# A third PSUM tile for the first MLP layer, a new order of fills, and earlier loads in a fused attention and MLP kernel

## The chip, the cores and the metric

One core of a Trainium2 chip. The metric is the device time of one execution in microseconds (us), the median of several. Executions fall into states: most agree closely, and some are several us longer; comparisons between kernels use the fast ones.

## The reference

Attention with a hash mask, then an MLP on its output, in float32:

```python
# q, k, v: (4 batches, 8 heads, 768, 64); proj: (64, 6)
q_bits = (q @ proj > 0); k_bits = (k @ proj > 0)     # 6 bits a token
mask   = bucket(q_bits)[:, None] == bucket(k_bits)[None, :]
attn   = softmax(where(mask, q @ k.T / 8, -1e9))
x      = (attn @ v) as (3072 tokens, 512)
h      = x @ w_in                                    # (3072, 2048): first layer
out    = (h * cos(h)) @ w_out                        # (3072, 512):  second layer
```

## The kernel before

The work runs in 192 units of attention, 48 a batch: TensorE (PE) makes scores in one of two tiles `s_ps` of PSUM (where its results land), ScalarE (ACT) takes the exp, PE multiplies by the values into `av_ps`. Two heads share one load ("pair"); pair n is loaded, cast, transposed and hashed some units before it is needed. Seven units into batch b, the *first layer* of batch b-1 runs: 16 rounds, one for each `ff`, of eight matmuls, cos on ACT, and the product h·cos on VectorE (DVE). The *second layer* of that batch, 96 matmuls of 512 columns in 6 row tiles of 16, is spread as "fills" over the following units and over the next first layer. The first layers of batches 1 and 2 are called the middle ones below: they have fills, that of batch 0 has none, that of batch 3 stands alone at the end.

```python
    s_ps = [psp.tile([P, 2, 512], FP32, ...) for i in range(2)]   # scores and first layer
    av_ps = [psp.tile([P, 512], FP32, ...) for i in range(2)]     # values, by head parity
    m_ps = [psp.tile([P, 512], FP32, ...) for i in range(2)]      # second layer, in turn
    ...
    def l1_ff(b, ff, hp):
        halves = hp if isinstance(hp, list) else [hp[:, c, :] for c in range(2)]
        for ft in range(NFT):
            for c in range(2):
                nc.tensor.matmul(out=halves[c][:, 0:C2], lhsT=win_t[ft][:, ff * P:(ff + 1) * P],
                    rhs=xT[(b, ft)][:, 3 * c:3 * c + 3, :], start=(ft == 0), stop=(ft == NFT - 1))
        ...                                    # ACT: cos; DVE: g = h * cos
    def l2_mm():
        b, qt, ff = l2q.pop(0)
        if ff == 0:
            state["m"] = 1 - state["m"]        # each row tile takes the other bank
        o_ps = m_ps[state["m"]]
        ...
        nc.tensor.matmul(out=o_ps, lhsT=g[:, qt * P:(qt + 1) * P], rhs=wout_t[ff],
            start=(ff == 0), stop=(ff == NFF - 1))
        if ff == NFF - 1:
            ...
            nc.vector.tensor_copy(out=ob, in_=o_ps)     # then the row tile goes out
            nc.sync.dma_start(out=dst, in_=ob)
    ...
            if n < NEARLY:                     # NEARLY = 5, UB = 48
                at(s0 + 2, lambda n=n: load(n + 2, nc.sync if n + 2 < NEARLY else nc.gpsimd))
            elif NEARLY < n < NP - 1:
                at(max(s0 - 1, UB + 8), lambda n=n: load(n + 1, nc.gpsimd))
    ...
    L1_AT = {UB * b + 7: b - 1 for b in range(1, B)}
    for u in range(U):
        score(h, jt); ...                      # exp, values, and what is due at this unit
        if b > 0:
            fill(2 if (u % 3 == 0) else 1)
        if u in L1_AT:
            bb = L1_AT[u]
            for ff in range(NFF):
                if bb == 0 and ff % 3 == 2:
                    hp = m_ps
                else:
                    hp = s_ps[state["rot"] % 2]
                    state["rot"] += 1
                l1_ff(bb, ff, hp)
                if bb == 0:
                    nc.gpsimd.tensor_copy(out=mark, in_=g_tiles[(0, ff)][:, 0, 0:1])
                    weights_out(ff)            # one of 16 w_out pieces
                if ff in (0, 1) and len(pend) > 0:
                    av_step()
                if bb > 0:
                    fill(2)
            l2_add(bb)
            fill(5)
```

Pairs from 5 on are transposed by DMA on the SyncE queue, while the loads come from GpSimd (POOL). DVE must copy the transposed keys (`kx<-qx`) before it makes the blocks of the next pair (`blkq`, `blkk`: its queries and keys, rearranged for the hash), and PE runs that hash between two units.

The softmax here doesn't subtract the row's maximum and nothing guards it: scores larger than these inputs give would overflow.

## Time and profile before

| | before |
|---|---|
| median, first three runs | 320.37 us (326.35, 320.37, 319.7) |
| profiled execution | 325.93 us, span 324.2 us, slow |
| PE busy in the profile | 309.6 us, 96% |
| middle first layers | 16 rounds of 1.73 us |
| longest wait of PE | 4.59 us, at 105 us |

The page of the profile: busy time of each engine, then the busy tenths and the granted clock of PE in 40 slices of the span.

```profile
span 324.2 us, 7617 instructions
...
PE 309.6 (96%) x3074; PEld 183.7 (57%) x3074; DVE 179.2 (55%) x376; ACT 231.1 (71%) x278; POOL 107.2 (33%) x180
...
PE   8899999999999499999999999999999999999995
...
PEclk9999999999999689999999999999999999999999
```

PE is full nearly everywhere. The exception is the 14th slice (from 105.4 us), where it is busy for less than half of the time; there and in the next its clock is below full. The same stretch in the chain of work that ended last, in order of time (start, duration, what):

```profile
95.37 12.17 DMA qx<-n16x
...
107.57 0.04 DVE kx L235
...
107.84 0.68 DVE ob L336
...
108.55 0.99 DVE blkq L143
...
109.59 0.85 PE m_ps L156 x2
```

Read downward, this is one wait: a DMA transpose lands at 107.5 us, only then can DVE copy the keys, empty an output bank and make the blocks of the next pair, and only then PE begins the hash. The timeline shows the parts on POOL (the natq load of pairs 7, 8, 9 and 10), SyncE (the transposes), DVE (the first key copy), PE and ACT; the columns are start, duration, engine, line, operation, tiles, count, and in brackets the idle time before and what ended it:

```profile
83.75 0.72 POOL L100 DMA_DIRECT2D natq<-in_q_dram  x1
...
85.87 0.74 POOL L100 DMA_DIRECT2D natq<-in_q_dram  x1
...
93.17 0.73 POOL L100 DMA_DIRECT2D natq<-in_q_dram  x1
...
101.22 0.72 POOL L100 DMA_DIRECT2D natq<-in_q_dram  x1
...
93.88 3.95 SPq L230 DMA_TRANSPOSE qx<-n16x  x2
...
105.53 0.35 DVE L235 COPY kx<-qx 64x768 f16<-64x768 f16 x1 [6.35 <-DMA qx<-n16x]
...
109.59 0.85 PE L156 MATMUL m_ps<-blkq,projblk 128*32 128x192 f32 x2 [4.59 <-DVE blkq L143]
...
95.81 10.00 ACT L250 ACTIVATE pt<-s_ps,exp_bias 128x768 f16<-128x768 f32 x12 [0.93 <-PE s_ps L244]
113.65 0.90 ACT L250 ACTIVATE pt<-s_ps,exp_bias 128x768 f16<-128x768 f32 x1 [7.84 <-PE s_ps L244]
```

An undisturbed hash costs ACT a pause of 0.93 us (the line at 95.81); this one costs 7.84. The second cause beside the wait is the clock, here a stretch of two us from the view of stretches (the columns are the stretch, its length, busy time of PE, PEld, DVE, ACT and POOL, then the granted clock, 0.50, and the DMA share and rate):

```profile
112.00:114.00 2.00, 2.00 (x11) 0.94 (x11) 1.80 (x10) 0.35 (x1) 0.00 (x0) 0.50 1.38 316
```

The records give half clock from 108.48 us for 6.83 us.

In the middle first layers PE is full in another way. This is the end of the first one in the timeline of before, PE's lines alone (L295 first layer, L323 second, L244 scores):

```profile
157.39 0.38 PE L323 MATMUL m_ps<-wout,g 128*128 128x512 f16 x1
...
157.88 1.46 PE L295 MATMUL s_ps<-xT,win 128*128 128x384 f16 x8
...
159.61 1.46 PE L295 MATMUL s_ps<-xT,win 128*128 128x384 f16 x8 [0.27 <-DVE g L309]
...
160.91 1.24 PE L323 MATMUL m_ps<-wout,g 128*128 128x512 f16 x5
...
161.98 0.49 PE L244 MATMUL s_ps<-qx,kx 128*128 128x512 f16 x2
...
163.12 0.48 PE L244 MATMUL s_ps<-qx,kx 128*128 128x512 f16 x2 [0.43 <-DVE g L309]
```

Up to here a round is 1.30 us of first layer and 0.43 us of two fills; the queue of fills is dry after 157.4 us. From then on the starts of PE's matmuls show three waits: 0.27 us for a tile before the 15th round (at 157.88 us, not marked), 0.44 us before the 16th (marked 0.27, because the ends of matmuls are modelled) and 0.60 us before the second score (marked 0.43).

### The profile page before, as it was taken

What the parts mean: (1) busy time and instruction counts of PE and PEld (TensorE: products, weight loads), DVE (VectorE), ACT (ScalarE), POOL (GpSimd) and SP (SyncE); (2) the same over time, 40 slices, a digit from 0 to 9 for tenths busy, and PEclk for the clock granted to TensorE, in tenths of its full rate; (3) what the DMA queues carried; (4) which work ended last, traced back from release to release, by engine and by line L of the source; (5) the groups of instructions that cost most, each with busy time, mean ns of one, the idle gap of its engine ahead of it and who ended that gap; (6) DMA issues with size and microseconds to landing.
All of it is one profiled execution on the core that took longest, in us unless ns stands there. A gap on an engine that the chain in (4) does not pass through costs nothing.

```text
span 324.2 us, 7617 instructions
## 1 busy us (share of the span) xinstructions
PE 309.6 (96%) x3074; PEld 183.7 (57%) x3074; DVE 179.2 (55%) x376; ACT 231.1 (71%) x278; POOL 107.2 (33%) x180
## 2 busy tenths in 40 slices
PE   8899999999999499999999999999999999999995
PEld 3577766565565166655556666655555665566442
DVE  3666458777571655655566574655666321377311
ACT  2799999977989088845598988854598995377000
POOL 4995295155885254500025754300020000000000
PEclk9999999999999689999999999999999999999999
DMA  7969959378899959700128889200124222100021
GB/s 248 335 117 229 264 122 117 62 101 104 195 256 147 212 89 225 205 4 32 38 53 229 165 154 217 66 1 32 39 52 103 64 57 58 65 2 0 34 98 66
DMA packets 45332, 37.74 MB, mean 116 GB/s; under 512 B 32264, under 2 KB 39200, under 8 KB 45296
## 3 DMA queue, kind: packets, MB, share of 16 engines
q1 hardware_dynamic: 38080, 19.35, 29.2%
q0 software_dynamic: 6576, 17.17, 22.8%
q10 hardware_dynamic: 640, 0.72, 0.7%
q8 instruction: 24, 0.39, 0.5%
q14 instruction: 12, 0.10, 0.2%
HBM read 27.26 MB, written 6.29 MB: 104 GB/s over the span
## 4 chain that ended last, share of the span: by engine, by line
PE 82%; ACT 7%; DMA 5%; DVE 4%; issue 1%; ACTq 0%; DVEq 0%
PE m_ps L323 24%; PE s_ps L295 21%; PE s_ps L244 17%; PE av_ps L266 9%; ACT pt L250 5%; PE m_ps L156 4%; DMA qx<-n16x 4%; PE m_ps L295 4%; DVE g L309 2%; ACT cos L307 1%; PE av_ps L259 1%; DMA natk<-in_k_dram 1%; PE m_ps L216 1%; DVE blkq L143 1%; PE av_ps L156 0%
## 5 line engine op out<-in xcount | busy, mean ns | idle before, releaser
L250 ACT ACTIVATE pt<-s_ps,exp_bias 128x768 f16<-128x768 f32 x192 | 160.1, 899 | 19.9 <-PE s_ps L244 18.6
L323 PE MATMUL m_ps<-wout,g 128*128 128x512 f16 x384 | 111.5, 381 | 0.3 <-DVE g L309 0.3
L244 PE MATMUL s_ps<-qx,kx 128*128 128x512 f16 (+1 forms) x384 | 94.5, 328 | 3.3 <-ACT pt L250 1.0
L295 PE MATMUL s_ps<-xT,win 128*128 128x384 f16 x432 | 77.5, 326 | 0.8 <-DVE g L309 0.5
L307 ACT ACTIVATE cos<-s_ps,cos_bias 128x768 f16<-128x768 f32 x54 | 48.6, 900 | 41.2 <-PE s_ps L295 41.2
L266 PEld LDWEIGHTS <-pt 128*128 128x128 f16 x1152 | 60.6, 98 | 24.0 <-issue 0.6
L309 DVE TENSOR_TENSOR g<-s_ps,cos 128x768 f16<-128x768 f32 x54 | 51.7, 958 | 38.5 <-ACT cos L307 38.4
L295 PEld LDWEIGHTS <-win 128*128 128x128 f16 x512 | 49.8, 98 | 37.7 <-issue 3.0
L266 PE MATMUL av_ps<-vx,pt 128*128 128x65 f16 x1152 | 66.0, 193 | 0.0
L244 PEld LDWEIGHTS <-kx 128*128 128x128 f16 x384 | 35.6, 98 | 31.6 <-issue 9.5
L323 PEld LDWEIGHTS <-g 128*128 128x128 f16 x384 | 34.0, 98 | 23.8 <-issue 3.9
L130 POOL CAST vx<-natv 128x768 f16<-128x768 f32 x16 | 13.2, 827 | 102.4 <-PE av_ps L266 95.2
L336 DVE COPY ob<-m_ps 128x512 f32<-128x512 f32 x23 | 15.7, 684 | 19.9 <-PE m_ps L323 19.7
L277 DVE RECIPROCAL rc<-av_ps 128x6 f32<-128x6 f32 x32 | 6.0, 189 | 33.8 <-PE av_ps L266 33.8
L156 PE MATMUL m_ps<-blkq,projblk 128*32 128x192 f32 (+1 forms) x152 | 15.6, 309 | 4.6 <-DVE blkq L143 4.6
L235 DVE COPY kx<-qx 64x768 f16<-64x768 f16 x22 | 13.0, 621 | 11.5 <-DMA qx<-n16x 11.2
L280 DVE TENSOR_TENSOR xn<-av_ps,rc 128x384 f16<-128x384 f32 x32 | 17.8, 558 | 1.4 <-DVE rc L277 0.3
L164 DVE TENSOR_SCALAR bh<-m_ps 128x192 f16<-128x192 f32 (+1 forms) x19 | 6.0, 315 | 20.4 <-PE m_ps L156 20.4
L125 POOL CAST n16x<-natq 128x768 f16<-128x768 f32 (+1 forms) x16 | 13.2, 824 | 9.8 <-DMA qx<-n16x 4.7
L132 POOL TENSOR_TENSOR vhalf<-natv 128x384 f32<-128x384 f32 x16 | 15.9, 995 | 0.0
L143 DVE STREAM_TRANSPOSE blkq<-natq 128x768 f32<-128x768 f32 x15 | 14.6, 975 | 0.3
L125 POOL CAST n16x<-natk 128x768 f16<-128x768 f32 (+1 forms) x16 | 13.0, 810 | 5.5 <-DMA natk<-in_k_dram 5.5
(67 smaller groups left out, 226.5 us busy)
## 6 DMA issues: line engine op xcount, KB each, us to landing
out_dram<-ob SPq DMA_DIRECT2D x23, 256.0 KB
natq<-in_q_dram POOLq DMA_DIRECT2D x11, 384.0 KB, 3.8
natk<-in_k_dram POOLq DMA_DIRECT2D x11, 384.0 KB, 5.4
natv<-in_v_dram POOLq DMA_DIRECT2D x11, 384.0 KB, 5.9
win<-in_moe_w_in_dram POOLq DMA_DIRECT2D x4, 512.0 KB, 7.0
wout<-in_moe_w_out_dram POOLq DMA_DIRECT2D x16, 128.0 KB, 2.9
natq<-in_q_dram SPq DMA_DIRECT2D x4, 384.0 KB
natk<-in_k_dram SPq DMA_DIRECT2D x4, 384.0 KB
```

The costliest lines, as they stand in the source:

```text
L125: engs[w].tensor_copy(out=o_, in_=i_)
L132: nc.gpsimd.tensor_tensor(out=half, in0=nv[:, :, 0:3, :], in1=nv[:, :, 3:6, :], op=ALU.add)
L143: nc.vector.transpose(out=blk[pr][w].rearrange("p h t c r -> p (h t c r)"), in_=nat[pr][w].rearrange("p h f -> p (h f)"))
L156: nc.tensor.matmul(out=hb[32 * j:32 * j + 32, :].rearrange("p (t r) -> p t r", r=32), lhsT=projblk[:, c].rearrange("p b i -> p (b i)"), rh ...
L244: nc.tensor.matmul(out=sp[:, c, 0:c1 - c0], lhsT=kx(pr)[:, hh, jt * P:(jt + 1) * P], rhs=qx(pr)[:, hh, c0:c1], start=True, stop=True)
L250: nc.scalar.activation(out=pt, in_=sp.rearrange("p c n -> p (c n)")[:, 0:S], func=ACTF.Exp, bias=exp_bias, scale=EXP_SCALE)
L266: nc.tensor.matmul(out=bank[:, qt * W:qt * W + D + 1], lhsT=pt[:, qt * P:(qt + 1) * P], rhs=vx_bufs[pr % 3][:, hh, jt, 0:D + 1], start=Fal ...
L280: nc.vector.tensor_tensor(out=xn[(b, ft)][:, :, hl % 2, :], in0=bank[:, :, 0:D], in1=rc.unsqueeze(2).to_broadcast([P, T, D]), op=ALU.mult)
L295: nc.tensor.matmul(out=halves[c][:, 0:C2], lhsT=win_t[ft][:, ff * P:(ff + 1) * P], rhs=xT[(b, ft)][:, 3 * c:3 * c + 3, :], start=(ft == 0) ...
L307: nc.scalar.activation(out=c_, in_=h_, func=ACTF.Sin, bias=cos_bias, scale=1.0)
L309: nc.vector.tensor_tensor(out=g_, in0=h_, in1=c_, op=ALU.mult)
L323: nc.tensor.matmul(out=o_ps, lhsT=g[:, qt * P:(qt + 1) * P], rhs=wout_t[ff], start=(ff == 0), stop=(ff == NFF - 1))
```

## The change

In the middle first layers the two output banks are in turn so that a row tile can be copied out while the next is begun. In the middle first layers the change keeps the second layer in one bank, and takes the other with `av_ps[0]`, idle at that point, as a third first-layer tile. It spreads fewer fills over the rounds (3, 3, 2, 2, then 1, instead of 2) and puts eight instead of five behind them. In the first layer of batch 0, w_out comes two pieces a round, in half the rounds, and load 7 follows at the ninth; it used to come after that layer.

```diff
+    ENDF = 8
+    L1F = lambda ff: (3,3,2,2)[ff] if ff<4 else 1
+    UF = lambda u: 2 if u % 3 == 0 else 1
...
-    state = {"m": 0, "rot": 0}
+    state = {"m": 0, "rot": 0, "hold": False}
...
-        if ff == 0:
+        if ff == 0 and not state["hold"]:
             state["m"] = 1 - state["m"]
...
-            elif NEARLY < n < NP - 1:
-                at(max(s0 - 1, UB + 8), lambda n=n: load(n + 1, nc.gpsimd))
+            elif NEARLY + 1 < n < NP - 1:
+                at(s0 - 1, lambda n=n: load(n + 1, nc.gpsimd))
...
-                fill(2 if (u % 3 == 0) else 1)
+                fill(UF(u))
             if u in L1_AT:
                 bb = L1_AT[u]
+                state["hold"] = bb > 0
                 for ff in range(NFF):
                     if bb == 0 and ff % 3 == 2:
                         hp = m_ps
+                    elif ff % 3 == 2:
+                        hp = [m_ps[1 - state["m"]], av_ps[0]]
                     else:
                         hp = s_ps[state["rot"] % 2]
                         state["rot"] += 1
                     l1_ff(bb, ff, hp)
                     if bb == 0:
                         nc.gpsimd.tensor_copy(out=mark, in_=g_tiles[(0, ff)][:, 0, 0:1])
-                        weights_out(ff)
+                        if ff < NFF // 2:
+                            weights_out(2 * ff)
+                            weights_out(2 * ff + 1)
+                        elif ff == NFF // 2:
+                            load(NEARLY + 2, nc.gpsimd)
                     if ff in (0, 1) and len(pend) > 0:
                         av_step()
                     if bb > 0:
-                        fill(2)
+                        fill(L1F(ff))
+                state["hold"] = False
                 l2_add(bb)
-                fill(5)
+                fill(ENDF)
```

## The prediction

> **What bounds the kernel now.** TensorE. The page has PE busy 309.6 of 324.2 us, and in the timeline matmul starts lie as close as the work allows: 215 ns for 512 columns, 162 ns for 384. ScalarE is close behind in attention: 12 exps take 10.0 us without a pause, then 0.93 us idle. In the middle first layers (133-163, 206-236 us) one ff takes 1.73 us: eight 384-column matmuls (1.30) plus two of the second layer (0.43). With two tiles PE is already full there. Its idle time in these stages, summed from matmul starts, is 1.3 us in the first (0.27 and 0.44 at the last two ff, where the second-layer queue has run dry, 0.60 before the second score after it) and 1.2 us in the second.
>
> The profiled run has one big loss besides: at 104.9 us PE waits 4.6 us for a hash, whose VectorE blocks stand behind a key copy that waited 6.35 us for the DMA transpose qx<-n16x. That was issued at 93.9 us, among loads issued at 83.8-88.0, 93.2 and 101.2 us. The granted clock is then 0.50 from about 108.5 to 115 us. I estimate the loss at 4.6 + half of 5.7 = 7.4 us. The Trainium skill ("TensorE: Matmul & The Clock Gate", "Why this matters for your kernels") asks for no PE gaps over about 3 us, or the clock falls to half; this trace agrees. The profiled execution took 325.93 us, fast ones 320: I take it that fast runs lose about 1.4 us here.
>
> **What the change does.**
> 1. Third tile in the two middle first layers. It removes no work (two half cos/products, 1.05/1.01 us against 0.90/0.96, are hidden). An ff now needs only one fill: 1.5 us. But fills are moved, not removed, and PE is full in attention too. Only idle time can go: the dry last ffs and, by eight fills instead of five, the wait before the scores: 1.3 + 1.2 us.
> 2. A new wait. The second layer has one bank in this stage. In program order a row tile ends after ff 2 (first middle layer) and ff 3 (second); the next waits for its copy, which stands behind that ff's product on VectorE. From durations (cos halves 1.05, product 1.0, copy 0.68) against the 1.30 us of PE until the next fill, I estimate 0.8 and 1.1 us. Net of 1 and 2: 0.6 us gained.
> 3. w_out in half the tiles, load 7 inside the first layer (about 73 instead of 83.8 us); load 8 then comes at 83, load 9 some 3 us earlier, so the transposes after 93.9 us meet less traffic and the key copy should end before 102 us, in time for the hash. I expect this wait to vanish: about 1.2 us in fast runs, 7 us in runs like the profiled one. This is the larger part.
>
> **Prediction.** 320.0 - 0.6 - 1.2 = 318.2 us, range 316.0 to 320.6. Faster by over 2%: 0.05; within 2%: 0.93; slower: 0.02.
>
> **What would show it.** Right: PE gap before the hash at 105 us under 1 us, no half clock after 20 us; natq loaded near 73 us; middle ffs about 1.5 us from the fifth on; one PE wait of about 1 us on the copy ob<-m_ps in each; none before the scores after them; PE work unchanged. Wrong: a gap still at 105 us or on a later transpose; ffs still 1.7 us.
>
> **What would make it wrong.** Fast runs may not have that wait at all (then 319.4). Earlier loads may collide with transposes elsewhere. The one-bank wait may be longer, or eight fills may hold back exps where ScalarE is the limit.

## The result, and the profile after

| | before | changed |
|---|---|---|
| median | 320.09 us (4 runs, 319.7 to 326.35) | 316.99 us (4 runs, 316.73 to 317.22) |
| ratio of the fast runs | | 0.9907 (95%: 0.9888 to 0.9927) |
| profiled execution | 325.93 us, slow | 316.94 us, fast |

A ratio is the mean time of one kernel's fast runs over that of the other's of the same rounds, so not quite the ratio of the medians. Here the means are 319.96 and 316.98 us: 3.0 us gained. None of the four runs was slow. All outputs are right. A run counts as slow when it is over 1.5% above the fastest, so runs of before at 322 and 323 us are among its fast ones in the experiments below.

The page of the changed kernel, the same lines:

```profile
span 315.2 us, 7635 instructions
...
PE 305.5 (97%) x3074; PEld 182.6 (58%) x3074; DVE 181.9 (58%) x386; ACT 232.3 (74%) x288; POOL 107.3 (34%) x180
...
PE   8899999999999999999999999989999999999995
...
PEclk9999999999999999999999999999999999999999
```

Lines from 90 on have moved down by three (the second layer is L326, the scores L247). The dip at 105 us and the missing clock there are gone. The timeline of the changed kernel at the same place: the natq loads of pairs 7 to 10, the transposes, the key copies and the blocks of the next pair on DVE, and the exps after that hash:

```profile
74.18 0.72 POOL L103 DMA_DIRECT2D natq<-in_q_dram  x1 [0.17 <-issue]
...
83.16 0.72 POOL L103 DMA_DIRECT2D natq<-in_q_dram  x1 [0.29 <-issue]
...
90.79 0.72 POOL L103 DMA_DIRECT2D natq<-in_q_dram  x1
...
101.73 0.72 POOL L103 DMA_DIRECT2D natq<-in_q_dram  x1
...
94.12 3.06 SPq L233 DMA_TRANSPOSE qx<-n16x  x2
...
99.72 1.75 DVE L238 COPY kx<-qx 64x768 f16<-64x768 f16 x2
...
102.10 0.98 DVE L146 STREAM_TRANSPOSE blkq<-natq 128x768 f32<-128x768 f32 x1
...
107.25 10.01 ACT L253 ACTIVATE pt<-s_ps,exp_bias 128x768 f16<-128x768 f32 x12 [0.93 <-PE s_ps L247]
```

The transposes are issued at the same time as before (94.1 against 93.9 us), but load 9 is now 2.4 us earlier, and load 7 is out of the way. The key copies begin at 99.72 us without a wait, where they waited until 105.5 and 107.6 us, and ACT's pause is the plain 0.93 us.

The timeline of the changed kernel in its first middle layer, where a row tile ends (PE's matmuls, the two halves of DVE's product and the copy of the tile):

```profile
131.53 0.59 PE L326 MATMUL m_ps<-wout,g 128*128 128x512 f16 x2
...
131.97 1.46 PE L298 MATMUL s_ps<-xT,win 128*128 128x384 f16 x8
...
132.19 0.56 DVE L312 TENSOR_TENSOR g<-m_ps,cos 128x384 f16<-128x384 f32 x1 [0.69 <-ACT cos L310]
132.66 0.55 DVE L312 TENSOR_TENSOR g<-av_ps,cos 128x384 f16<-128x384 f32 x1
...
133.13 0.68 DVE L339 COPY ob<-m_ps 128x512 f32<-128x512 f32 x1
...
133.87 0.59 PE L326 MATMUL m_ps<-wout,g 128*128 128x512 f16 x2 [0.43 <-DVE ob L339]
```

Here is the price of the one bank: the two matmuls at 131.53 us end a row tile; its copy stands in DVE's queue behind the two halves of the product and ends at 133.8 us; PE, done with the next round at 133.3 us, waits. The list of PE's waits in the changed kernel has this one and its like in the second middle layer (us in all, times, longest; the ends of matmuls are modelled, and between starts the two waits are 0.60 and 1.08 us):

```profile
PE m_ps L326 <- DVE ob L339: 1.3, 2, 0.9
```

PE's own view of the whole run, from the starts of matmuls, is the best ledger. A segment goes from one first layer to the next. "Idle" is what lies between two starts beyond the usual distance (162 ns after a first-layer, 215 after a second-layer, 109 after the second score matmul), counted where it is over 20 ns, without the hash. The fast profile of before is from the experiments below.

```
segment, us             before, slow   before, fast   changed   second-layer matmuls in it
first layer 0 to 1             73.80          67.36     66.67   69, now 72
first layer 1 to 2             72.70          72.70     71.55   96, now 94
first layer 2 to 3             72.99          72.99     72.36   123, now 122
idle in 1 to 2                  2.02           2.03      1.30
idle in 2 to 3                  2.13           2.13      1.68
```

With 0.215 us for each matmul that moved, fast before against changed, the first segment gained 0.69 + 0.65 = 1.34 us, the two middle ones 1.15 - 0.43 = 0.72 and 0.63 - 0.22 = 0.42 us. The idle time agrees: 0.73 and 0.45.

### The profile page after: what moved, and what is told of

Same layout as the page of the kernel before. It is cut to its first block, busy times and chain, and to the rows that moved or that the text cites. A ratio compares the mean times of both kernels' runs of the same rounds, so it can differ in the third digit from the quotient of the medians.

```text
span 315.2 us, 7635 instructions
## 1 busy us (share of the span) xinstructions
PE 305.5 (97%) x3074; PEld 182.6 (58%) x3074; DVE 181.9 (58%) x386; ACT 232.3 (74%) x288; POOL 107.3 (34%) x180
## 4 chain that ended last, share of the span: by engine, by line
PE 88%; ACT 6%; DVE 3%; issue 1%; DVEq 0%; ACTq 0%
PE m_ps L326 27%; PE s_ps L247 19%; PE s_ps L298 17%; PE av_ps L269 9%; PE m_ps L298 6%; ACT pt L253 5%; PE m_ps L159 4%; PE av_ps L298 2%; PE av_ps L262 1%; PE s_ps L365 1%; PE m_ps L219 1%; DVE g L312 1%; ACT cos L310 1%; DVE blkq L146 1%; PE av_ps L159 1%
## 5 line engine op out<-in xcount | busy, mean ns | idle before, releaser
L326 PE MATMUL m_ps<-wout,g 128*128 128x512 f16 x384 | 111.1, 379 | 1.7 <-DVE ob L339 1.3
L247 PE MATMUL s_ps<-qx,kx 128*128 128x512 f16 (+1 forms) x384 | 93.8, 326 | 2.5 <-ACT pt L253 1.0
L298 PE MATMUL s_ps<-xT,win 128*128 128x384 f16 x352 | 62.9, 326 | 0.1
L310 ACT ACTIVATE cos<-s_ps,cos_bias 128x768 f16<-128x768 f32 x44 | 39.6, 900 | 30.5 <-PE s_ps L298 30.5
L312 DVE TENSOR_TENSOR g<-s_ps,cos 128x768 f16<-128x768 f32 x44 | 42.1, 957 | 34.1 <-ACT cos L310 34.0
L247 PEld LDWEIGHTS <-kx 128*128 128x128 f16 x384 | 35.3, 97 | 30.0 <-issue 7.5
L326 PEld LDWEIGHTS <-g 128*128 128x128 f16 x384 | 33.9, 98 | 25.0 <-issue 4.2
L298 PE MATMUL m_ps<-xT,win 128*128 128x384 f16 x120 | 27.7, 326 | 0.0
L310 ACT ACTIVATE cos<-m_ps,cos_bias 128x384 f16<-128x384 f32 x30 | 16.3, 577 | 9.4 <-PE m_ps L298 8.3
L312 DVE TENSOR_TENSOR g<-m_ps,cos 128x384 f16<-128x384 f32 x30 | 15.7, 551 | 3.1 <-ACT cos L310 2.5
L238 DVE COPY kx<-qx 64x768 f16<-64x768 f16 x22 | 15.3, 729 | 3.0 <-DMA qx<-n16x 2.7
```

Source lines behind the costliest of these rows:

```text
L247: nc.tensor.matmul(out=sp[:, c, 0:c1 - c0], lhsT=kx(pr)[:, hh, jt * P:(jt + 1) * P], rhs=qx(pr)[:, hh, c0:c1], start=True, stop=True)
L310: nc.scalar.activation(out=c_, in_=h_, func=ACTF.Sin, bias=cos_bias, scale=1.0)
L312: nc.vector.tensor_tensor(out=g_, in0=h_, in1=c_, op=ALU.mult)
```

## The experiments

The theory: most of the gain is the wait at 105 us, which has a long form (with half clock, the slow runs) and a short form (the fast runs), and which earlier loads end; the third tile gives nothing by itself, but lets fills move, and their new places take out some idle time and add two bank waits. The rival: the third tile makes the first layers faster and that is the gain; the loads matter in slow runs at most. Four, four and three kernels ran on three chips, with five rounds each beside the kernel before.

### 1. The kernel before again

No edit.

> The kernel before, unchanged, against itself: how often it is slow, and a second profile. If the slow state is a wait of over 3 us before the hash near 105 us followed by half clock, a slow profile shows it again and costs 6 us; a fast profile (about 320 us) should show the same wait at 1 to 3 us and no half clock. Rival: the fast run has no wait there at all, and the 1.8 us of the change's 3.1 us that the first layers do not explain come from elsewhere.

Measured: 319.34 us median; of 17 runs of this kernel, 7 took 323 to 331 us and the other ten 319.0 to 319.8. The profile was fast (319.1 us). Its timeline (the two key copies of pair 7 on DVE, and the exps after that hash on ACT) shows the short form:

```profile
101.11 0.60 DVE L235 COPY kx<-qx 64x768 f16<-64x768 f16 x1 [2.31 <-DMA qx<-n16x]
102.94 0.35 DVE L235 COPY kx<-qx 64x768 f16<-64x768 f16 x1 [1.23 <-DMA qx<-n16x]
...
107.63 10.01 ACT L250 ACTIVATE pt<-s_ps,exp_bias 128x768 f16<-128x768 f32 x12 [2.21 <-PE s_ps L244]
```

The key copies come at 101.1 and 102.9 us, late by less, and ACT's pause is 2.21 us, 1.28 over the plain one. So even this fast run, 0.3 us above the fastest of all, loses 1.28 us there, and there is no half clock. Over all, 20 of 45 executions of before took 323 us or more. Of those whose clock is on record, all of 321.9 us or more had a mean clock of 0.984 to 0.995, all of 320.4 us or less one of 0.997 to 1.0: the half clock goes with the slow state. The slow profiles are that of the section before the change and that of experiment 6.

### 2. The loads alone

```diff
 (the kernel before, with the two hunks of the change about w_out and load 7)
-                        weights_out(ff)
+                        if ff < NFF // 2:
+                            weights_out(2 * ff)
+                            weights_out(2 * ff + 1)
+                        elif ff == NFF // 2:
+                            load(NEARLY + 2, nc.gpsimd)
 ... (and the hunk of the later loads)
```

> Only the w_out pieces and the early load on the kernel before; two tiles, old fills. My theory (the DMA part is the larger one): 318.0 to 318.5 us, 1.5 to 2 us under before's fast runs, no run slow, no wait before the hash near 105 us. Rival (the third tile makes the gain): within 0.5 us of before's fast runs.

Measured: 318.2 us (317.61 to 320.17), ratio 0.9949 (0.9884 to 1.0015), no run slow. PE has no wait before that hash, and the first segment is 66.08 us against 67.36. As the theory has it; the interval by itself does not exclude 1, since the fast runs of before scatter up to 323 us.

### 3. The tile and the fills alone

```diff
 (the changed kernel, with those two hunks undone)
+                        weights_out(ff)
-                        if ff < NFF // 2:
-                            weights_out(2 * ff)
...
+            elif NEARLY < n < NP - 1:
+                at(max(s0 - 1, UB + 8), lambda n=n: load(n + 1, nc.gpsimd))
```

> Only the third tile, the held bank and the new fills; w_out one piece a tile and the load as before. My theory: 318.5 to 319.5 us in fast runs, 0.8 to 1.3 us under before, and slow runs of about 325 us as before has. Rival (the tile makes the gain): 317 us, like the changed kernel.

Measured: 318.53 us, from 317.13 to 319.95 and one slow run of 324.54; ratio 0.9932 (0.9865 to 1.0). The best runs are lower than I expected, 1.9 us under the best of before. The profile (a best run) says why: ACT's pause at that hash is 1.43 us there, not 2.21. The three extra fills after first layer 0 push the units back by 0.6 us, while the second key copy comes no later (102.76 against 102.94 us), so the two parts of the change meet in the same wait. The runs at 319.5 and over and the slow one remain: this part seems to shorten the wait sometimes (one profile shows it), it does not end it. By the ratios it gained no less than the loads alone did (0.9932 against 0.9949, with intervals that overlap), so in fast runs the gain does not divide into two separate parts.

### 4. No fill in the round after a row tile

```diff
-    L1F = lambda ff: (3,3,2,2)[ff] if ff<4 else 1
+    L1G = {1: (3, 3, 2, 0, 2, 2), 2: (3, 3, 2, 2, 0, 2)}
...
-                        fill(L1F(ff))
+                        fill(L1G[bb][ff] if ff < 6 else 1)
```

> The changed kernel, but no second-layer matmul in the ff after the one that ends a row tile; the two that this leaves out come one ff later. If PE's waits of 0.60 and 1.08 us at 133 and 206 us are for the copy of the one bank, they go: 315.3 us, 1.7 under the changed kernel. If PE is held there by something else (the first-layer tile or cos), the wait turns up elsewhere and the time stays at 317.

Measured: 314.99 us (314.71 to 315.4), ratio 0.983 (0.9778 to 0.9882; whether that is more than 2% is unclear). The changed kernel on other chips took 316.97 and 316.99. The bank waits are gone. The timeline of this version at the place where the changed kernel waited at 133 us:

```profile
131.21 0.59 PE L326 MATMUL m_ps<-wout,g 128*128 128x512 f16 x2
...
131.65 2.76 PE L298 MATMUL s_ps<-xT,win 128*128 128x384 f16 x16
...
132.81 0.68 DVE L339 COPY ob<-m_ps 128x512 f32<-128x512 f32 x1
...
134.25 0.59 PE L326 MATMUL m_ps<-wout,g 128*128 128x512 f16 x2
```

PE goes straight through two rounds (16 matmuls from 131.65 us) while the copy runs, and the next fill at 134.25 us finds its bank empty. The segments are 70.95 and 71.28 us, 0.60 and 1.08 shorter than in the changed kernel, to the hundredth what the starts had shown as waits. That the third tile is what allows this (with two there is no third round to go on with) is argued and was not run.

### 5. The changed kernel again, on the chip of experiments 6 to 8

No edit.

> The changed kernel again, on the chip of these runs: 316.8 to 317.3 us, no slow run, and 2.1 us under the fastest runs of before (1.28 us for the wait before the hash, about 0.8 us for the first layers). Where before's fast runs scatter above their fastest, the ratio is larger than that.

Measured: 316.97 us, five runs from 316.61 to 317.3 and one of 319.0; ratio 0.9921 (0.9873 to 0.997). The 319.0 was not profiled, and what it waited for is open; its mean clock was 1.0, so it was no half clock.

### 6. w_out earlier, load 7 where it was

```diff
 (the kernel before)
-                        weights_out(ff)
+                        if ff < NFF // 2:
+                            weights_out(2 * ff)
+                            weights_out(2 * ff + 1)
```

> The kernel before with w_out two pieces a tile, but load 7 still after the first layer. If it is load 7 that pushes the later loads into the transposes, this brings under 0.5 us, the exp pause at the hash near 106 us stays over 1.5 us, and some runs stay slow. Rival (the last w_out pieces, issued to 83 us, are what is in the way): 317.9 us and no slow run, like both loads changes together.

Measured: 320.59 us (319.61 to 325.56), ratio 1.0033 (0.9969 to 1.0097). No gain, and one of the six runs is slow. The profile is of that run, with the wait in its long form (4.94 us before the hash); the first exp after that hash in its timeline:

```profile
113.77 0.90 ACT L250 ACTIVATE pt<-s_ps,exp_bias 128x768 f16<-128x768 f32 x1 [8.19 <-PE s_ps L244]
```

### 7. Load 7 earlier, w_out where it was

```diff
 (the kernel before)
                         weights_out(ff)
+                        if ff == NFF // 2:
+                            load(NEARLY + 2, nc.gpsimd)
...
-            elif NEARLY < n < NP - 1:
-                at(max(s0 - 1, UB + 8), lambda n=n: load(n + 1, nc.gpsimd))
+            elif NEARLY + 1 < n < NP - 1:
+                at(s0 - 1, lambda n=n: load(n + 1, nc.gpsimd))
```

> The kernel before with load 7 inside the first layer at ff 8, w_out still one piece a tile. If load 7 is the cause: 317.9 us, exp pause at the hash 0.93 us, no slow run. Rival (w_out is the cause, or w_out now lands too late behind load 7): 319 us or more, or a wait for w_out in the second layer near 85 us.

Measured: 318.03 us (317.87 to 318.53), ratio 0.9945 (0.9907 to 0.9983), no slow run; the first segment is 66.08 us, as with both load edits. So load 7 does it alone, and w_out in half the rounds gives nothing by itself. With experiment 5, on the same chip: 318.03 to 316.97 us, 1.06 us for the tile and the fills when the wait is already gone.

### 8. The output banks one round earlier in first layer 0

```diff
 (the kernel of experiment 4)
-                    if bb == 0 and ff % 3 == 2:
+                    if bb == 0 and ff % 3 == 1:
                         hp = m_ps
-                    elif ff % 3 == 2:
+                    elif bb > 0 and ff % 3 == 2:
```

> The version with the skipped fill, and in the first of the first layers the output banks serve ff 1, 4, ... 13 instead of 2, 5, ... 14, so that the last product from them is over before the second layer begins. PE's wait of 0.47 us at 80.3 us should go: 314.5 us. If that wait only moves to the scores behind it, the time stays at 315.0.

Measured: 315.23 us (314.74 to 317.28), ratio 0.9865 (0.9821 to 0.9909). PE's wait at 80 us is gone, but the time is that of experiment 4 (on another chip): an expectation missed. The profiles show where the 0.47 us went. The first segment is 66.34 us instead of 66.68. Counted from the start of the first layer, the exps begin after 23.74 us instead of 24.05, so 0.31 us arrives there. ACT keeps the rest: its last cos begins at 80.65 us, then comes the switch of its table, 1.28 us, and the exps at 82.86 us follow without idle time, where in experiment 4 ACT still waited 0.32 us for PE. The profiled run then loses the gain elsewhere: its first layer began 0.31 us later (59.12 against 58.81 us), and its middle segments are 0.15 and 0.13 us longer. Whether 0.3 us would show over more runs on one chip is open. It still is 1.7 us under the changed kernel of the same chip (experiment 5).

### 9. The third tile with the old fills

```diff
-    ENDF = 8
-    L1F = lambda ff: (3,3,2,2)[ff] if ff<4 else 1
+    ENDF = 5
+    L1F = lambda ff: 2
```

> The changed kernel with the third tile and its loads, but with the old fills (two per ff, five at the end). If the gain of the middle layers lies in the fills and not in the tile, this is slower: the second layer's row tile then ends inside a burst of two, and PE waits some 2.5 us for the copy of its one bank in each middle layer (one copy behind one product), the wait before the scores returns (0.5 us each): about 320.5 us, 3.5 over the changed kernel. Rival (the tile alone makes the gain): 317 us or less.

Measured: 321.34 us (320.08 to 322.65), ratio 1.0021 (0.9956 to 1.0087). The tile with the old fills loses more than all that the loads gain. The row tile ends inside a burst, and PE waits about 2 us for the bank in each middle layer; the timeline of the second one:

```profile
209.59 0.38 PE L326 MATMUL m_ps<-wout,g 128*128 128x512 f16 x1
...
211.25 0.68 DVE L339 COPY ob<-m_ps 128x512 f32<-128x512 f32 x1
...
211.98 0.50 PE L326 MATMUL m_ps<-wout,g 128*128 128x512 f16 x1 [2.01 <-DVE ob L339]
```

After this wait the clock is half for 3.41 us (from 212.10 us); after the like one in the first middle layer, 1.95 us, it is not. Their lengths hardly differ, but their places may matter. In the profiles each change of the clock lies a whole multiple of 3.413 us after the one before (3.41, 6.83, 102.40, 208.21 us). On this grid the wait of 2.01 us lies inside one step (208.69 to 212.10 us), while the one of 1.95 us is cut at 137.01 us into 1.14 and 0.82 us. Two cases do not settle whether the idle time within a step or the length of the wait decides.

The wait before the scores did not return as expected (0.14 us each by the starts, not 0.5); PE waited 0.46 and 0.39 us before the five fills instead. Three of the six runs have a mean clock of 0.993 to 0.995 and take 321.9 to 322.7 us; the other three, at 0.998 to 1.0, take 320.1 to 320.8, and even these are above the fastest runs of before.

### 10. The new fills with two tiles

```diff
-                    elif ff % 3 == 2:
-                        hp = [m_ps[1 - state["m"]], av_ps[0]]
...
-                state["hold"] = bb > 0
```

> The changed kernel with its fills and loads, but two first-layer tiles and two output banks in turn. If the tile is what lets an ff get by with one fill, PE now waits for the product of the ff two before, some 0.2 us per ff with one fill (period about 1.7 instead of 1.5 us): 24 times, about 5 us, less the 1.7 us of bank waits that go: 320 us. Rival (one fill is enough with two tiles): 315.3 us, like the skipped fill.

Measured: 320.0 us (319.6 to 322.21), ratio 0.9993 (0.9921 to 1.0065). A round stays at 1.71 to 1.78 us instead of 1.51, and PE's idle time before the first-layer matmuls is 2.36 and 2.64 us in the two segments. Two of its cos in the timeline of ACT:

```profile
138.02 0.90 ACT L310 ACTIVATE cos<-s_ps,cos_bias 128x768 f16<-128x768 f32 x1 [0.83 <-PE s_ps L298]
139.73 0.90 ACT L310 ACTIVATE cos<-s_ps,cos_bias 128x768 f16<-128x768 f32 x1 [0.81 <-PE s_ps L298]
```

So neither the fills nor the tile work alone: with the loads as in the changed kernel they take 3.0 and 4.4 us more than it did (316.97 us, on another chip).

### 11. Load 9 after the casts of pair 8

```diff
 (the kernel before)
             elif NEARLY < n < NP - 1:
-                at(max(s0 - 1, UB + 8), lambda n=n: load(n + 1, nc.gpsimd))
+                at(s0 + 1 if n == 8 else max(s0 - 1, UB + 8), lambda n=n: load(n + 1, nc.gpsimd))
```

> The kernel before with one order changed: load 9 comes after the casts of pair 8 instead of before them, so it no longer runs beside the DMA transposes of pair 7; load 7 and w_out as before. If load 9 beside these transposes makes the wait, the key copies of pair 7 end near 100 us and the exp pause at the hash near 106 us is 0.93 us; loads 9 and 10 then come together at 101 us and may make a like wait one pair later (near 117 us). Rival (it is loads 7 and 8 that are in the way): the key copies still end at 103 us or later and the pause near 106 us stays over 1.5 us.

Measured: 323.17 us (319.06 to 325.22, two runs slow), ratio 1.0023 (0.9922 to 1.0123). The profile (322.95 us) shows what the theory said: the key copies of pair 7 come without a wait and the pause near 106 us is 0.93 us; loads 9 and 10 are issued together from 100.9 us, the transposes of pair 8 at 104.4 us run beside them, and the wait stands one pair later. The exps after the two hashes in the timeline of this version:

```profile
106.46 10.00 ACT L250 ACTIVATE pt<-s_ps,exp_bias 128x768 f16<-128x768 f32 x12 [0.93 <-PE s_ps L244]
122.41 8.39 ACT L250 ACTIVATE pt<-s_ps,exp_bias 128x768 f16<-128x768 f32 x10 [5.95 <-PE s_ps L244]
```

Loads 7 and 8 were as in the kernel before, so in this profile it is not they that hold up the transposes of pair 7 directly. Load 7 does it by its place in the row: with load 7 alone earlier (experiment 7), load 9 is issued at 90.23 us, against 92.69 in the fast profile of before, and is ahead of the transposes (93.14 us).

## Why the prediction was right or wrong

The time, 316.99 us, lies in the range (316.0 to 320.6), and "within 2%" came true. Point by point:

- **The wait at 105 us vanishes: right; that it is the larger part: only just, in fast runs.** The wait vanished, load 7 came at 74.2 us, load 9 came 2.4 us earlier (I said some 3), and 46 executions of the seven kernels with the early load had none of 323 us or more. The estimate of 1.4 us for fast runs, made only from the difference between the slow profile and the fast times, was measured as 1.28 in the profile of a fast run. That it came so close is in part luck: by the first segment, against that of the loads alone (66.08 us), the slow profile lost 7.72 us, not 7.4, and the fast profile is of 319.1 us, not 320. As the larger part, the wait is plain in slow runs (7.72 us). In fast ones it is 1.28 us against the 1.14 of the middle segments, and which edit seems to bring more depends on the order in which they are made (experiment 3).
- **Its size in the mean was too small.** I booked 1.2 us; load 7 alone gives a ratio of 0.9945, 1.8 us. The fast runs of before are not one time: they scatter upward from 318.8. The wait has more than one length (ACT's pause is 2.21 us in the fast profile, 7.84 in the slow one); that the runs between have lengths between is not shown. Measured against fast times of 320.0 I expected 1.8 us and 3.0 came; this term is half of what I missed.
- **Fills are moved, not removed; only idle time can go: right.** The tile with the old fills costs 4.4 us, the fills without the tile 3.0. The rounds take 1.51 us, as said.
- **The new bank waits: right in kind, place and number, a little large.** 0.60 and 1.08 us, where I had 0.8 and 1.1. Experiment 4 took exactly these out.
- **Net 0.6 us for tile and fills: too small.** It is 1.14 us by the segments, 1.06 by the runs of experiments 5 and 7. Of the old idle time I had counted 1.3 + 1.2 us, and 1.33 + 1.53 went: I had left out gaps under 60 ns, 0.30 us together. The new waits cost 1.68 us, not 1.9. The gaps of 0.09 to 0.10 us between fills and scores, 0.67 and 0.47 us in the two segments, stayed as they were. This is the other half.
- **No wait before the scores: right.** "PE s_ps <- DVE g", 0.8 us in the list of before, is not in that of after. Eight fills did not hold back exps by more than they did work.

How the half clock comes about was taken from the Trainium skill, "TensorE: Matmul & The Clock Gate", "What's actually happening": the clock is passed at half rate after an idle window of about 3.4 us. The trace agrees in the lengths, 3.41 and 6.83 us, but not in the threshold (see the last section). The page "DMA: Bandwidth & Descriptors", section "Issuing engines are not separate DMA queues", says that DMAs started by the scalar, sync or gpsimd engine run on the same 16 DMA engines and interleave. Experiments 7 and 11 agree: moving a load of POOL's queue by a few us sets whether a transpose of SyncE's queue lands in time. How the two share an engine no run here shows.

Open: why the wait differs so much from run to run of one kernel, and the one run of 319.0 us of the changed kernel.

## What to carry to other kernels

Where an engine is full on average, a new buffer gives nothing until work is moved into the time that it frees; judge the two together, and look for the new wait that a taken buffer leaves behind: here a skipped fill after each row tile gave another 1.7 us. When runs of one kernel fall into two states, look for one wait whose length varies, in a fast profile too, before calling the slow state noise: moving one load 10 us ahead took the slow state away. And a wait of PE is worth its length only as far as PE is what the next stage waits for: of 0.47 us that vanished at 80 us, 0.31 reached ACT, and the time of the runs did not show it.

## What the Trainium skill lacked or had wrong

- "TensorE: Matmul & The Clock Gate", "Why this matters for your kernels": no PE gaps over about 3 us. Here PE waits of 2.01 and 2.81 us were each followed by 3.41 us of half clock; waits of 4.59 and 4.94 us by 6.83 us. One of 1.95 us was not. In these runs only waits under 2 us were free of it; where a wait lies on the clock's steps of 3.413 us may matter too (experiment 9).
- "DMA: Bandwidth & Descriptors", "Rules for kernel authors", says that a transpose next to ordinary DMAs needs nothing, in a row about silently corrupted results. For the result that held in all runs. For the time it did not: two transposes issued at 93.88 us, beside loads, let the last key copy start at 107.57 us, against no wait at 99.72 us with those loads a little earlier. The page gives no cost for this.
- No page that I used warns that one wait of varying length before PE, with the clock behind it, makes the same kernel appear in two states (319 us, and 323 to 331 us in 20 of 45 runs).
